# Weights fetched apart from rows, plans ahead of scatters, and places converted when due, in an FFT-then-mixture-of-experts kernel

## The chip, the cores and the metric

The kernel runs on one core of one Trainium2 chip. The metric is the device time of one execution in microseconds (us); less is better. A core has five engines with in-order queues of their own, and they synchronise through semaphores: PE multiplies matrices (PEld is its weight load), DVE and ACT do elementwise work, POOL issues the indirect DMAs here, and SP issues the plain DMAs. All DMAs share 16 DMA engines.

## What is computed

A 2-D Fourier transform of 8 batches of 2496 x 256 numbers, of which the real part is kept, and behind it a top-1 mixture of experts: each of the 19,968 rows goes to the one of 8 experts with the largest gate logit, through two matrix products with a ReLU between, and is scaled by its gate weight.

```
batch, seq, dim = (8, 2496, 256);  N, D, E, F = (19968, 256, 8, 1024)
x = real(fft(fft(x, axis=1), axis=2)).reshape(N, D)
logits = x @ w_gate
e = argmax(logits, axis=1)
gate_w = softmax(logits)[e]
for each expert e, its rows:  y = relu(x @ w1[e]) @ w2[e]
out = gate_w[:, None] * y
```

## The kernel before

Work goes batch by batch through three stages, and the stages of different batches are woven into each other.

*First stage* (`first(b)`): x comes in three pieces per batch (`load`, SP), is folded on DVE (L290 to L301), multiplied by tables on PE (tile s), copied by ACT, and written to a DRAM tensor Td. `regroup` reads it back as tile t4.

*Second stage* (`second(b)`): further products (tiles p, zz) give the transformed rows and their gate logits. After each half batch `route` picks the expert and counts, so that each row gets a place in a DRAM tensor Xs in which every expert has a region: `pf` is the place as a float, `pi` as an integer (L447, L448). For each of the 10 slices of 128 rows it appends an entry to the list `waiting`. `send()` takes one entry from it and issues one indirect DMA on POOL (L230), which writes 128 rows to their places. A batch has 20 such scatters.

*Plan*: once a batch is routed, `close(b)` runs `plan` (L469): some 25 small DVE instructions on one partition, which turn the counts per expert into a table `tab` of blocks: from which row each block starts, and which expert it belongs to. Batch b's blocks are "round" b: two of 256 rows and four of 128 in the first round, four of 256, then three of 512, then five of 512 in each, and in the last round five of 512, seven of 256 and up to 21 of 128 rows.

*Expert blocks* (`experts`, L623): for each block, `fetch` (L517) reads the block's start row and its expert from `tab` into registers of SP and issues three DMAs on SP: the rows (tile xb, from Xs) and the two weights of its expert (w1_sb and w2_sb, both shown as w_sb, 1 MB each). Each has three buffers. `turn` transposes the rows on PE (tile pt) and DVE copies them to xT. The first product (ph, into hT through ReLU on ACT and DVE in turn) and the second (py, scaled by ACT into y, scattered to the output by POOL) follow. The transposes of the next block stand in PE's order between the output products of the current one. Blocks of 512 rows from round 3 on (`halved`) do their first product by seven smaller ones (`seven`, L577, tiles a to e), with extra DVE sums; `Left` makes the sums of weights for it, four DVE instructions (L546).

*What sets the order.* The program is written out in the order in which the engines run it (`manual_schedule`). The loop at L804 weaves: for each batch b from 1 on, `work` yields the blocks of round b-1 in steps (a step has a weight w and says whether PE has its fill), and `side = mixed(b)` is batch b's second stage with the next batch's first stage. After each step that is not "full", side work becomes due at TICKS * w / (SHARE * open_), with TICKS 32 and SHARE 0.65: about so much that 32 steps are done after 65% of the round. For batches below LATE = 4 each side step is followed by one `send()`. From batch 4 on `send()` comes when an allowance `room`, which grows by w per step, reaches ROOM = 1.2.

In `mixed`, a loop waits until `waiting` is empty, and only then does `close(b)` plan the batch. In `experts`, `fetch_some` fetches up to three blocks ahead at the start of a block, and up to two ahead after its first product; it needs the plan and nothing else, since a planned batch has all its scatters issued. DMAs of SP are issued in order, so a fetch of rows that waits for scatters to land keeps the fetches behind it waiting.

Rows that a block reads are ordered behind the scatters of its round's batches by dependency groups (`sent`, `taken`, L235 to L243).

Of the kernel before, what the change touches and what calls it, by code (L numbers as in the profile page):

```python
# [15 lines left out]
ALU = mybir.AluOpType  # L16
# [19 lines left out]
E, F = 8, 1024  # L36
# [145 lines left out]

TICKS = 32
LATE = 4
SHARE, ROOM = 0.65, 1.2
WARM = 16
MOST = max(k for now in rounds() for _, k, _ in now)

# [21 lines left out]
def kernel(ctx: ExitStack, tc, x, w_gate, w1, w2, out):  # L210
    nc = tc.nc
# [51 lines left out]
    con, k = {}, 0  # L263
# [147 lines left out]
    def route(b, h, rows, lg):  # L411

        nonlocal base

        def small(name, *dims, dt=F32):
            return sp.tile([128, *dims], dt, tag=name, name=name)

        mx, eq, v = small("mx", NSL), small("eq", NSL, E), small("v", NSL)
        vec.reduce_max(mx[:], lg[:], axis=AX_X)
        vec.tensor_tensor(eq[:], lg[:], bc(mx[:], 2, E), op=ALU.is_equal)  # L420
        vec.tensor_tensor(eq[:], eq[:], bc(con["rev"][:], 1, NSL), op=ALU.mult)
        vec.reduce_max(v[:], eq[:], axis=AX_X)
# [24 lines left out]
        vec.reduce_sum(pf[:], pos[:], axis=AX_X)  # L447
        vec.tensor_tensor(pi[:], pf[:], con["far"][:, h], op=ALU.add)  # L448
        nxt = cp.tile([128, E], F32, tag="base", name="base", bufs=2)
        vec.tensor_tensor(nxt[:], rk[:, NSL], base[:], op=ALU.add)  # L450
        base = nxt
        for s in range(NSL):
            waiting.append((b, pi[:, s:s + 1], rows[:, s]))

    waiting = deque()

    def send():

        if waiting:
            b, idx, rows = waiting.popleft()  # L460
            sent(put_row(Xs, idx, rows, E * CAP - 1, "xs"), b)


# [50 lines left out]
        yield  # L514
        tabs[b, size, last] = tab

    def fetch(b, size, tab, i):  # L517
        n = size // 128
        row = nc.sync.value_load(tab[:, 0, i:i + 1], min_val=0, max_val=ROWS - size)
        ev = nc.sync.value_load(tab[:, 1, i:i + 1], min_val=0, max_val=E - 1)  # L520
        xb = bp.tile([128, BIG // 128, W], F32, tag="xb", name="xb", bufs=3)
        taken(nc.sync.dma_start(out=xb[:, 0:n].rearrange("p t c -> p (t c)"),
                                in_=Xs[ds(row, size)].rearrange("(p t) c -> p (t c)", t=n)), b)
        w1_sb = bp.tile([128, 2, F], F32, tag="w1", name="w1_sb", bufs=3)
        nc.sync.dma_start(out=w1_sb[:], in_=w1[ds(ev, 1)].rearrange("o p c f -> p (o c) f"))
        w2_sb = bp.tile([128, FC, D], F32, tag="w2", name="w2_sb", bufs=3)
        nc.sync.dma_start(out=w2_sb[:], in_=w2[ds(ev, 1)].rearrange("o p c d -> p (o c) d"))
        return xb, w1_sb, w2_sb

    add, sub = ALU.add, ALU.subtract  # L530

# [22 lines left out]
        vec.tensor_tensor(o[2], b21, o[1], op=sub)  # L554
        return b11, b21, b22, o[2], o[0], o[1], b12

    def turn(b, size, got):


        xb = got[0]  # L560
        xT = bp.tile([128, 2, BIG], F32, tag="xT", name="xT", bufs=1)
        n = min(size // 128, 2)
        for h in range(-(-size // 256)):
            pt = pse.tile([128, 2, n, 128], F32, tag="e", name="pt")
            for c in range(2):
                for t in range(n):
                    nc.tensor.transpose(pt[:, c, t], xb[:, 2 * h + t, c * 128:(c + 1) * 128], ident[:])  # L567
            vec.tensor_scalar(xT[:, :, 256 * h:256 * h + 128 * n], pt[:].rearrange("p c t k -> p c (t k)"),  # L568
                              con["alt"][:], None, op0=ALU.mult)
            yield xT  # L570
        if halved(b, size):
            th = size // 2
            xs = bp.tile([128, 3, th], F32, tag="xs", name="xs", bufs=1)
            r = right(xs, *(xT[:, c, k * th:(k + 1) * th] for c in range(2) for k in range(2)))
            yield r
# [47 lines left out]
    def experts(todo):  # L623
# [1 line left out]

        got, xT, used, left = [], None, None, None

        @contextmanager  # L630
        def needed(last, at, o):
# [11 lines left out]

        def fetch_some(k, most=3):

            while k + len(got) < len(todo) and len(got) < most and todo[k + len(got)][:3] in tabs:
                b, size, last, at = todo[k + len(got)]
                got.append(fetch(b, size, tabs[b, size, last], at))

        for k, (b, size, last, at) in enumerate(todo):  # L650
            n, m = size // 128, BIG // size
            if not k:
                while todo[0][:3] not in tabs:
                    yield 0, False
                fetch_some(0)
                for _ in range(9):
                    yield 0, False
                for xT in turn(b, size, got[0]):
                    pass
            fetch_some(k)  # L660
            xb, w1_sb, w2_sb = got.pop(0)
# [4 lines left out]
            hT = bp.tile([128, FC, BIG], F32, tag="hT", name="hT", bufs=1)  # L666
            more = None
            if follow and got and halved(follow[0], follow[1]):
                more = Left(got[0][1])
# [16 lines left out]
            if follow:  # L686
                while follow[:3] not in tabs:
                    yield 0, False
                fetch_some(k + 1, 2)
                turned = turn(*follow[:2], got[0])  # L690
                if halved(*follow[:2]):
                    left = more or Left(got[0][1])
# [26 lines left out]
    def woven(*parts):  # L719
        parts = list(parts)  # L720
        while parts:
            for p in list(parts):
                if next(p, p) is p:
                    parts.remove(p)
                else:
                    yield

    def close(b):

        for size, k, last in rounds()[b]:  # L730
            yield from plan(b, size, k, last)

    def ahead_of(b):

        yield from first(b)
        regroup(b, 0)
        regroup(b, 1)

    def mixed(b):

        one, two = (ahead_of(b + 1) if b + 1 < B else iter(())), second(b)
        for _ in range(3):
            next(one, None)
            yield
        for k, _ in enumerate(two):
            if k % 2:
                next(one, None)
            yield
        while waiting:
            next(one, None)  # L750
            yield
        yield from woven(close(b), one)

    vec.memset(ones[:], 1.0)
    act.dma_start(out=con["w1"][:, 0:4], in_=waves[:, 0:4])
# [11 lines left out]
    vec.memset(warm[:], 0.0)  # L767
    act.activation(warm[:], warm[:], ACTF.Exp)

    tabs = {}  # L770
    todo = in_order()
    for _ in first(0):
        pass
# [22 lines left out]
    for k, _ in enumerate(second(0)):  # L796
        if k % 2 == 0:
            next(early, None)
        send()
    while waiting:  # L800
        next(early, None)
        send()
    work = experts(todo)
    for b in range(1, B):  # L804

        side, done, due, room = mixed(b), 0, 0.0, 0.0
        if b == 1:
            side = woven(close(0), chain(early, side))
        blocks = [(size, k * size / BIG, halved(b - 1, size)) for size, k, _ in rounds()[b - 1]]
        total = sum(k * (15 if seven_ else 16) for _, k, seven_ in blocks)  # L810
        open_ = sum(k * (8 if seven_ else 16) for _, k, seven_ in blocks)
        while done < total:
            w, full = next(work)
            done += w
            if not full:
                due += TICKS * w / (SHARE * open_) if w else 1
            while due >= 1:
                next(side, None)
                due -= 1
                if b < LATE or not w:  # L820
                    send()
            room = min(room + w, 2)
            if b >= LATE and room >= ROOM:
                send()
                room -= ROOM
        for _ in side:
            send()
# [52 lines left out]
```

## Time and profile before

| what | us |
|---|---|
| median of the runs (lowest) | 1332.57 (1330.49) |
| the profiled execution | 1364.11 |
| its span, first to last instruction | 1362.3 |
| TensorE (PE) busy | 1284.0 |
| first expert product (ph) starts | 92.1 |
| POOL busy with 160 scatters of rows to Xs | 158.7 |
| POOL busy with 163 scatters of output rows | 159.4 |

The profiled execution is 31.5 us longer than the median of the runs, so sums made in the profile are in its own us. The span in 40 slices of 34 us, in tenths of busy time, with the clock that the throttle granted to TensorE and the DMA engines' share:

```profile
PE   6668899899899999999999999999999999999998
POOL 0235215134113411044112521144131111111111
PEclk9869999899999999999999999999999999999999
DMA  8759866644535542454423542232442227777784
```

TensorE is below 90% in the first five slices, where the first batch passes through the first two stages before any block can start, and in a few slices later. The groups of instructions that the change concerns, with count, total busy us, mean ns, and idle time of the engine before them and what ended it:

```profile
L230 POOL DMA_INDIRECT out_dram<-y,ro x163 | 159.4, 978 | 890.6 <-ACT y L702 823.9
L230 POOL DMA_INDIRECT Xs<-rows,pi x160 | 158.7, 992 | 140.1 <-issue 64.3
L567 PE MATMUL pt<-table,xb 128*128 128x128 f32 x326 | 53.3, 279 | 10.8 <-DMA xb<-Xs 9.9
w_sb<-in_moe_w_dram SPq DMA_DIRECT2D x132, 1024.0 KB
xb<-Xs SPq DMA_DIRECT2D x28, 516.0 KB
```

### The profile page before, as it was taken

The numbers are of one execution on the slowest core, as the hardware profiler recorded it, in microseconds if no ns is written. First come the engines' busy times: TensorE is split into PE (matmuls) and PEld (weight loads), VectorE is DVE, ScalarE is ACT, GpSimd is POOL, SyncE is SP. The second block draws the span as 40 slices with busy tenths as digits, with TensorE's granted clock in tenths as the row PEclk, the third lists the DMA queues.
The fourth block names the chain that finished last, engine by engine and source line by source line (L and its number), as shares of the span: only waits on it lengthen the run. The fifth ranks groups of instructions, "written<-read, shape, count | busy, mean of one in ns | idle before, by whom it ended". The sixth has DMA issues, their size and how long they took to land.

```text
span 1362.3 us, 18852 instructions
## 1 busy us (share of the span) xinstructions
PE 1284.0 (94%) x6655; PEld 1103.7 (81%) x6655; DVE 581.0 (43%) x1533; ACT 368.9 (27%) x806; POOL 326.1 (24%) x335
## 2 busy tenths in 40 slices
PE   6668899899899999999999999999999999999998
PEld 4557888576688888887888878888888889999887
DVE  4553244332456465655366554555545421111211
ACT  1322132132134332432234223332223221111111
POOL 0235215134113411044112521144131111111111
PEclk9869999899999999999999999999999999999999
DMA  8759866644535542454423542232442227777784
GB/s 239 250 214 315 294 239 191 250 127 145 226 93 177 195 170 97 134 177 137 174 109 117 201 184 93 94 131 68 177 182 107 89 96 275 260 259 272 267 318 187
DMA packets 63099, 249.62 MB, mean 183 GB/s; under 512 B 10057, under 2 KB 24883, under 8 KB 43420
## 3 DMA queue, kind: packets, MB, share of 16 engines
q1 hardware_dynamic: 46231, 203.33, 42.6%
q0 software_dynamic: 15888, 42.14, 8.5%
q10 hardware_dynamic: 885, 2.94, 0.7%
q8 instruction: 54, 0.88, 0.3%
q14 instruction: 41, 0.34, 0.1%
HBM read 194.97 MB, written 54.83 MB: 183 GB/s over the span
## 4 chain that ended last, share of the span: by engine, by line
PE 87%; DVE 4%; DMA 3%; issue 3%; another core or an unknown queue 1%; ACT 1%; POOL 0%; SPq 0%; POOLq 0%; DVEq 0%; ACTq 0%
PE py L215 40%; PE ph L215 14%; PE a L215 6%; PE c L215 6%; PE p L215 6%; PE b L215 3%; PE d L215 3%; PE pt L567 3%; PE s L215 3%; PE e L215 3%; DMA xq<-in_x_dram 1%; DMA Td<-t 1%; DMA xb<-Xs 1%; DVE hT L606 0%
## 5 line engine op out<-in xcount | busy, mean ns | idle before, releaser
L215 PE MATMUL py<-w_sb,hT 128*128 128x256 f32 x2560 | 580.2, 381 | 6.3 <-DVE hT L682 4.0
L215 PEld LDWEIGHTS py<-w_sb,hT 128*128 128x128 f32 x2560 | 479.2, 191 | 68.0 <-DVE hT L682 4.6
L230 POOL DMA_INDIRECT out_dram<-y,ro x163 | 159.4, 978 | 890.6 <-ACT y L702 823.9
L215 PE MATMUL ph<-xT,w_sb 128*128 128x128 f32 (+2 forms) x1216 | 221.2, 337 | 8.7 <-issue 4.1
L702 ACT ACTIVATE y<-py,xb 128x256 f32<-128x256 f32 x163 | 77.1, 473 | 521.6 <-PE py L215 505.2
L215 PEld LDWEIGHTS ph<-xT,w_sb 128*128 128x128 f32 x1216 | 178.0, 192 | 40.4 <-issue 19.7
L230 POOL DMA_INDIRECT Xs<-rows,pi x160 | 158.7, 992 | 140.1 <-issue 64.3
L682 DVE TENSOR_SCALAR hT<-ph 128x512 f32<-128x512 f32 x63 | 43.5, 691 | 298.5 <-issue 204.1
L600 DVE TENSOR_TENSOR u<-p,b 128x512 f32<-128x512 f32 x50 | 34.4, 688 | 182.3 <-PE b L215 141.1
L215 PE MATMUL a<-xT,w_sb 128*128 128x256 f32 x400 | 103.3, 381 | 5.0 <-ACT p L597 4.3
L215 PEld LDWEIGHTS a<-xT,w_sb 128*128 128x128 f32 x400 | 75.4, 190 | 17.3 <-ACT p L597 5.5
L568 DVE TENSOR_SCALAR xT<-pt,table 128x512 f32<-128x512 f32 (+1 forms) x94 | 63.2, 673 | 46.1 <-PE pt L567 46.1
L403 DVE COPY lg<-p 128x16 f32<-128x16 f32 x80 | 13.9, 173 | 141.9 <-ACT zs L400 129.9
L215 PE MATMUL s<-xq,w 104*112 104x256 f32 (+2 forms) x208 | 61.7, 421 | 12.0 <-DVE xq L292 11.9
L684 ACT ACTIVATE hT<-ph 128x512 f32<-128x512 f32 x63 | 37.6, 597 | 114.2 <-PE ph L215 78.8
L215 PE MATMUL p<-table,zz 128*128 128x145 f32 (+1 forms) x320 | 58.5, 308 | 10.1 <-issue 5.1
L610 ACT ACTIVATE hT<-a 128x512 f32<-128x512 f32 x50 | 29.9, 597 | 137.2 <-PE a L215 117.0
L215 PEld LDWEIGHTS p<-table,t 120*128 120x128 f32 x352 | 53.7, 203 | 12.6 <-issue 9.2
L567 PE MATMUL pt<-table,xb 128*128 128x128 f32 x326 | 53.3, 279 | 10.8 <-DMA xb<-Xs 9.9
L215 PE MATMUL p<-table,t 120*128 120x120 f32 (+1 forms) x352 | 56.1, 287 | 4.4 <-issue 4.4
L567 PEld LDWEIGHTS pt<-table,xb 128*128 128x128 f32 x326 | 38.6, 142 | 25.8 <-DMA xb<-Xs 11.1
L215 PE MATMUL c<-xT,ws 128*128 128x256 f32 x200 | 52.3, 384 | 7.2 <-DVE hT L606 7.2
(113 smaller groups left out, 1266.3 us busy)
## 6 DMA issues: line engine op xcount, KB each, us to landing
w_sb<-in_moe_w_dram SPq DMA_DIRECT2D x132, 1024.0 KB
xq<-in_x_dram SPq DMA_DIRECT2D x24, 896.0 KB
xb<-Xs SPq DMA_DIRECT2D x28, 516.0 KB
Td<-t SPq DMA_DIRECT2D x18, 448.0 KB
t<-Td SPq DMA_DIRECT2D x8, 768.0 KB
t<-Td SPq DMA_DIRECT2D x8, 640.0 KB
xb<-Xs SPq DMA_DIRECT2D x13, 258.0 KB
xb<-Xs SPq DMA_DIRECT2D x25, 129.0 KB
```

The lines of the kernel that those rows point to most:

```text
L215: nc.tensor.matmul(o, lhsT=lhsT, rhs=rhs, start=start, stop=stop, **kw)
L230: return unordered(pool.indirect_dma_start(out=dst, out_offset=bass.IndirectOffsetOnAxis(ap=idx, axis=0), in_=rows, in_offset=None, bounds ...
L403: vec.tensor_copy(lg[:, k:k + 2], p3[:, NY:NY + 2 * E].rearrange("p (m e) -> p m e", m=2))
L567: nc.tensor.transpose(pt[:, c, t], xb[:, 2 * h + t, c * 128:(c + 1) * 128], ident[:])
L568: vec.tensor_scalar(xT[:, :, 256 * h:256 * h + 128 * n], pt[:].rearrange("p c t k -> p c (t k)"), con["alt"][:], None, op0=ALU.mult)
L600: vec.tensor_tensor(u2[:], p1[:], b[:], op=add)
L610: act.activation(h11, a[:], ACTF.Relu)
L682: vec.tensor_scalar(o, ph[:], 0.0, None, op0=ALU.max)
L684: act.activation(o, ph[:], ACTF.Relu)
L702: act.activation(y[:], py[:], ACTF.Copy, scale=xb[:, i, D + 1:D + 2])
```

## The change

1. *Rows and weights are fetched by two functions.* `fetch_weights` needs only the plan. `fetch_rows` needs also that all scatters of the batch are issued, which a new set `whole` tells. `fetch_some` fetches both in turn, and weights may be at most one block ahead of rows.
2. *Plans come ahead of scatters.* `mixed` no longer waits for `waiting` to be empty before `close(b)`; a new step `through(b)` behind it waits and adds b to `whole`. A block whose batch is not whole makes `experts` yield until it is; for batches below 4 such a yield issues all scatters that wait.
3. *Places when due.* From batch 4 on, `route` leaves the place as a float (pf), and `send()` lets ACT convert one column of it to pi just before it issues the scatter.
4. *Two constants.* SHARE goes from 0.65 to 0.6, and from batch 4 on the allowance for scatters grows by 0.75 w instead of w in steps that are not full.

```diff
-SHARE, ROOM = 0.65, 1.2
+SHARE, ROOM = 0.6, 1.2
...
-        vec.tensor_tensor(pi[:], pf[:], con["far"][:, h], op=ALU.add)
+        vec.tensor_tensor(pf[:] if b >= LATE else pi[:], pf[:], con["far"][:, h], op=ALU.add)
...
-            waiting.append((b, pi[:, s:s + 1], rows[:, s]))
+            waiting.append((b, pf[:, s:s + 1], pi[:, s:s + 1], rows[:, s]))
...
-            b, idx, rows = waiting.popleft()
+            b, place, idx, rows = waiting.popleft()
+            if b >= LATE:
+                act.copy(idx, place)
             sent(put_row(Xs, idx, rows, E * CAP - 1, "xs"), b)
...
-    def fetch(b, size, tab, i):
+    def fetch_rows(b, size, tab, i):
         n = size // 128
         row = nc.sync.value_load(tab[:, 0, i:i + 1], min_val=0, max_val=ROWS - size)
-        ev = nc.sync.value_load(tab[:, 1, i:i + 1], min_val=0, max_val=E - 1)
         xb = bp.tile([128, BIG // 128, W], F32, tag="xb", name="xb", bufs=3)
         taken(nc.sync.dma_start(out=xb[:, 0:n].rearrange("p t c -> p (t c)"),
                                 in_=Xs[ds(row, size)].rearrange("(p t) c -> p (t c)", t=n)), b)
+        return xb
+
+    def fetch_weights(tab, i):
+        ev = nc.sync.value_load(tab[:, 1, i:i + 1], min_val=0, max_val=E - 1)
         w1_sb = bp.tile([128, 2, F], F32, tag="w1", name="w1_sb", bufs=3)
...
-        return xb, w1_sb, w2_sb
+        return w1_sb, w2_sb
...
-            while k + len(got) < len(todo) and len(got) < most and todo[k + len(got)][:3] in tabs:
+            while max(len(got), len(xbs)) < min(most, len(todo) - k) or len(xbs) < len(got):
+                n = len(xbs)
+                b, size, last, at = todo[k + n]
+                if (b, size, last) in tabs and b in whole:
+                    xbs.append(fetch_rows(b, size, tabs[b, size, last], at))
+                elif n < len(got):
+                    break
                 b, size, last, at = todo[k + len(got)]
-                got.append(fetch(b, size, tabs[b, size, last], at))
+                if (b, size, last) not in tabs:
+                    break
+                if len(got) <= n:
+                    got.append(fetch_weights(tabs[b, size, last], at))
...
                 while todo[0][:3] not in tabs:
                     yield 0, False
+                fetch_some(0, 1)
+                while b not in whole:
+                    yield 0, True
                 fetch_some(0)
...
                 fetch_some(k + 1, 2)
-                turned = turn(*follow[:2], got[0])
+                while follow[0] not in whole:
+                    yield 0, follow[0] < LATE
+                fetch_some(k + 1, 2)
+                turned = turn(*follow[:2], xbs[0])
...
+    def through(b):
+
+        while waiting and waiting[0][0] == b:
+            yield
+        whole.add(b)
...
-        while waiting:
-            next(one, None)
-            yield
         yield from woven(close(b), one)
+        yield from through(b)
...
-    while waiting:
-        next(early, None)
-        send()
     work = experts(todo)
...
-            side = woven(close(0), chain(early, side))
+            side = woven(chain(close(0), through(0)), chain(early, side))
...
             done += w
+            if full and not w:
+
+                while waiting:
+                    send()
+                whole.add(b - 1)
...
-            room = min(room + w, 2)
+            room = min(room + (w if full else 0.75 * w), 2)
```

More of the change, by code (lines that the diff above doesn't have):

```diff
@@ L555, in right, with turn @@
         return b11, b21, b22, o[2], o[0], o[1], b12
-    def turn(b, size, got):
-        xb = got[0]
+    def turn(b, size, xb):
         xT = bp.tile([128, 2, BIG], F32, tag="xT", name="xT", bufs=1)
@@ L623, in experts @@
     def experts(todo):
-        got, xT, used, left = [], None, None, None
+        xbs, got, xT, used, left = [], [], None, None, None
         @contextmanager
@@ L657, in experts @@
                     yield 0, False
-                for xT in turn(b, size, got[0]):
+                for xT in turn(b, size, xbs[0]):
                     pass
             fetch_some(k)
-            xb, w1_sb, w2_sb = got.pop(0)
+            xb, (w1_sb, w2_sb) = xbs.pop(0), got.pop(0)
             turned = iter(())
@@ L668, in experts @@
             if follow and got and halved(follow[0], follow[1]):
-                more = Left(got[0][1])
+                more = Left(got[0][0])
             if halved(b, size):
@@ L689, in experts @@
                 fetch_some(k + 1, 2)
-                turned = turn(*follow[:2], got[0])
+                while follow[0] not in whole:
+                    yield 0, follow[0] < LATE
+                fetch_some(k + 1, 2)
+                turned = turn(*follow[:2], xbs[0])
                 if halved(*follow[:2]):
-                    left = more or Left(got[0][1])
+                    left = more or Left(got[0][0])
             for i in range(n):
@@ L768 @@
     act.activation(warm[:], warm[:], ACTF.Exp)
-    tabs = {}
+    tabs, whole = {}, set()
     todo = in_order()
```

## The prediction

> **What bounds the kernel now.** I read the page's engine shares first, then TensorE's waits, then busy time by stretch, then the timeline of the stretches in which TensorE stands still.
>
> ```profile
> span 1362.3 us, 18852 instructions
> PE 1284.0 (94%) x6655; PEld 1103.7 (81%) x6655; DVE 581.0 (43%) x1533; ACT 368.9 (27%) x806; POOL 326.1 (24%) x335
> PE pt L567 <- DMA xb<-Xs: 9.9, 2, 6.6
> PE c L215 <- DVE hT L606: 7.2, 9, 1.7
> PE a L215 <- ACT p L597: 4.3, 3, 1.7
> ```
>
> TensorE (PE) is busy 94% of the span and no matmul is removed or added, so the change can only win back idle time and time at a lowered clock: at most the other 6%, 78 us. Most of that is out of reach. The first expert matmul (ph) starts at 92.1 us, after the first transform, a hand-over through DRAM, and 20 scatters of 1.28 us each on POOL. The second to fourth lines (engine, what waits, who releases it: total us, times, longest) show two waits that the diff names: transposes (pt) that wait for rows, and products that wait for ACT or DVE.
>
> The rows first. This is the end of the blocks that run while batch 2 is scattered:
>
> ```profile
> 239.56 0.97 POOL L230 DMA_INDIRECT Xs<-rows,pi  x1 [0.30 <-issue]
> 242.07 0.37 SPq L522 DMA_DIRECT2D xb<-Xs  x1
> 242.64 0.37 SPq L525 DMA_DIRECT2D w_sb<-in_moe_w_dram  x1
> 245.50 1.11 PE L567 MATMUL pt<-table,xb 128*128 128x128 f32 x4 [6.60 <-DMA xb<-Xs]
> ...
> 240.00:245.00 5.00, 0.00 (x0) 0.00 (x0) 0.00 (x0) 0.00 (x0) 0.54 (x1) 0.73 0.49 157
> 245.00:250.00 5.00, 4.50 (x15) 3.83 (x16) 0.75 (x1) 0.00 (x0) 0.00 (x0) 0.59 1.00 420
> 350.00:355.00 5.00, 4.07 (x13) 3.37 (x14) 0.75 (x1) 0.00 (x0) 0.00 (x0) 0.66 1.01 410
> ```
>
> Timeline lines give start, duration, engine and, in brackets, the idle time before; stretch lines give length, busy time of PE, PEld, DVE, ACT, POOL, granted clock, DMA share, GB/s. The last scatter ends at 240.5, the rows are asked for at 242.1 and the weights behind them, the transposes start at 245.5, and PE, which had no other work, lost 6.6 us and then ran at a granted clock of 0.59. The same happens a round later, at 347.6 (3.3 us, clock 0.66).
>
> Now the small waits later on:
>
> ```profile
> 628.08 0.97 POOL L230 DMA_INDIRECT Xs<-rows,pi  x1 [0.30 <-issue]
> 629.36 0.97 POOL L230 DMA_INDIRECT Xs<-rows,pi  x1 [0.30 <-issue]
> 630.63 0.97 POOL L230 DMA_INDIRECT Xs<-rows,pi  x1 [0.30 <-issue]
> 633.16 0.58 ACT L597 COPY p<-a 128x512 f32<-128x512 f32 x1 [1.54 <-PE c L215]
> 633.80 1.13 PE L215 MATMUL a<-xT,w_sb 128*128 128x256 f32 x4 [1.66 <-ACT p L597]
> ...
> 427.00:1000.00 573.00, 558.97 (x2833) 485.58 (x2832) 310.85 (x765) 187.72 (x396) 158.53 (x162) 1.00 0.42 147
> ```
>
> From 427 to 1000 us PE idles 573.0 - 559.0 = 14.0 us. Every idle spot over 0.2 us (near 448, 477, 604, 633, 760, 790, 912, 940, 997) stands within or at most 5 us behind a run of four or more scatters back to back on POOL, during which ACT and DVE start 1 to 2 us after the matmul they are put down to has ended. That is a correlation; why a run of scatters holds ACT and DVE up the trace does not say.
>
> **The change part by part.** Reference: the profiled execution, 1364.1 us (span 1362.3), which is 2.4% above the median of the runs, 1332.57. I sum in the profile's us and scale.
>
> 1. *Plan ahead of the scatters, rows and weights apart, side work earlier (0.65 to 0.60).* No instruction of weight is added: the same plans, the same 132 weight and 66 row transfers. What moves is order. In the emitted order the second half of batch 2 is routed 3.4 us of PE work sooner (151.2 to 147.8 on a count of matmul columns at 216 ns per 256 columns and two passes, the pace of py in the chain: 3.46 us for 16), its plan 11 us sooner, and only one scatter is left after the next-to-last output row instead of three plus one. Three scatters less there are 3 x 1.28 = 3.8 us (1.28 from start to start, as 628.08 to 629.36 above); I take the last scatter to end 3.5 to 5 us sooner, near 236. The rows need 3.4 us from issue (242.07 to 245.50) and 1.6 from scatter end to issue: 236 + 5 = 241 against 238.9, when PE arrives. The wait falls from 6.6 to about 2.1, **4.5 us**. The restart ran 16 py in 4.75 us instead of 3.46 and pt in 0.9 instead of 0.44: another **1.8**. Who is late next: nobody behind PE, since the first weights now go before the rows.
> A rule of the Trainium skill speaks against this one: DMA: Bandwidth & Descriptors, "Anatomy of one DMA", says each DMA engine shares itself in turn between the queues that have work. The early weights (2 x 1024 KB) then share with the last scatters. The row beside it: 220 to 230 us already shows a DMA share of 0.95 to 0.97, but 230 to 240 only 0.21 to 0.26, and 420 GB/s was reached at 245. Two MB at that pace are 5 us; asked for near 224, they are through before the last scatters of 233 to 236. With the row I charge nothing; by the rule in its worst form the scatters end 2 us later and this part gives 4.3 instead of 6.3. I keep 6.3 and put 2 us in the range.
>
> 2. *Next round boundary (347.6).* The plan ran at 337.9 to 346, after the scatters, on DVE between hT copies; rows were asked for at 347.3. Now they are asked for at the start of the last block, as soon as the scatters land (about 341). PE arrives at 347.6: the 3.3 us wait goes, and 0.95 + 0.52 us of waits for hT at 337 and 341.7, which stood in the plan's neighbourhood, by half. Clock: 1.7 us (half speed for 3.4 us). Sum **5.7**. Here TensorE: Matmul & The Clock Gate, "Part 1: The HAM clock gate", gives about 3.4 us of idleness as what halves the clock: by it alone a 3.3 us wait might cost no clock, and this part would be 4.0. The measured 0.66 after just this wait decides. The 2.1 us left at the first boundary should cost none: waits of 1.7 and 2.3 us near 125 and 131 left the granted clock at 1.00.
>
> 3. *Places when due, and the slower allowance (0.75 per step outside the seven products).* From batch 4 on a scatter cannot start before ACT has converted its place, and ACT reaches that conversion in step with its own work. Runs of six (emitted together after an output row in before) become groups of three, one, two, one with 2 to 3 us of matmuls between. Of the 14.0 us idle in 427 to 1000, 2.1 us (at 996 to 999) belong to the pad scatters, which are not touched. Of 11.9 I take two thirds: **8.0**. Bounds: 0 if the runs are not the cause, 11.9 if all.
> Cost: 80 copies of one column on ACT. Nearest row: the copies of 5 or 6 columns at L367, 170 ns: 80 x 0.17 = 13.6 us of ACT, which is 67% idle in this stretch (187.7 of 573). Behind each copy in ACT's order stand the copy of a and the Relus that PE needs; bounds 0 and 13.6, I take **-1.0**. POOL now waits for ACT where it waited for DVE; the outputs queued behind it have six y buffers. DVE is unchanged (pf instead of pi, 170 ns).
>
> 4. *The first block.* Its weights are asked for when its plan is ready (about 72 us, DMA share 0.2 to 0.3 then) instead of at 86.7. Rows still wait for the last scatter (85.9). They landed 3.9 us after issue beside 2 MB of weights; alone I take 2.4: **1.5**. Bounds 0 and 2.
>
> Sum: 6.3 + 5.7 + 8.0 - 1.0 + 1.5 = 20.5 us; 1364.1 - 20.5 = 1343.6, times 1332.57/1364.1 = **1312 us**.
>
> **The rivals.**
> *More than that (chance 0.27).* From 120 to 150 us PE is busy 21.95 of 30 us, 8.05 lost, at a DMA share of 0.89, with ACT and DVE idle up to 10.9 us for a reason that the trace puts to "remote". Two MB of weights moved from 87 to 72 thin out the queue of transfers that leads up to it. If that was the cause, 20.5 + 8.05 = 28.5 us: 1335.6, scaled 1305. Against: the transfers of this stretch itself are issued at 121 to 139 and are the same.
> *Only the boundaries (0.17).* POOL's runs only coincide with the waits, or the grouped copies let the runs happen again: part 3 gives 0 to -1. 12.5 us are left: 1351.6, scaled 1320. This is also the case in which the change does not spread what it means to spread.
> *ACT turns into the bound (0.06), slower.* Place: the seven products of batches 4 to 7, where product a waits for ACT's copy of a (already 4.3 us in three waits). Price: 80 copies, each in front of such a copy or of a Relu. Before its own cost the sum is 21.5: from 0.27 us per copy (21.5/80) all of it is gone, which is over its own 170 ns and so needs queueing as well; or, with part 3 void, from 0.17 (13.5/80). At 0.35 us each and part 3 void, 28 - 13.5 = 14.5 us more: about 1379, scaled 1347. For it: ACT is in order, and its chain is what PE waits for. Against: 67% idle.
>
> **How the numbers follow.** The forecast itself has 0.50. Faster by over 2% (below 1305.9; 2% is about what a measurement of this kernel can tell from no change) holds most of the first rival and the upper end of the forecast, where bursts give all 11.9 and the restart costs nothing: 0.25 + 0.10 = 0.35. Slower by over 2% (above 1359): only the end of the last rival, 0.03. Within: 0.62. Range: the first rival with some more of the waits before 92 us, 1297, to a little beyond "only the boundaries", 1327.
>
> **What would show it.** The wait of pt for xb near 239 should be under 3 us and the one near 348 gone, both with granted clock near 1.0. The sum of PE idle in the five later rounds should fall from 14.0 to about 6, with no more than three scatters back to back there. ACT busy should rise by about 14 us with its waits by PE unchanged. If the stretch 120 to 150 is also full, the first rival is right. I am wrong if PE's idle spots remain though the scatters are spread, or if a new wait of PE for ACT p appears.

## The result, and the profile after

Kernel before and changed kernel ran in turn on one chip, six executions each. The changed kernel's median is 1321.03 us (1318.04 to 1322.44), that of before there 1331.38 us (five of the six from 1329.07 to 1332.57; one took 1944.71 us, and the record does not say why). The ratio is 0.9925, with a 95% interval of 0.9908 to 0.9941: 10.4 us less, a gain that the interval separates from zero. The forecast was 1312 us; the measured time lies inside its range, 9 us from its middle, and the gain is about half of the 20 us that were forecast.

The profiles tell of a larger step than the runs do. The changed kernel's profiled execution, 1322.44 us, is one of its six. The profiled execution of before, 1364.11 us, is none of the six beside it; it took 32.7 us more than their median, and on which chip it ran is not on record. So the spans differ by 41.6 us and the medians by 10.4. Three quarters of what the two traces show as won is no gain of this comparison, and the section on the experiments is mostly about finding out what it is.

The page of the changed kernel: span, busy time of each engine, and TensorE and its granted clock in 40 slices.

```profile
span 1320.7 us, 19014 instructions
PE 1277.2 (97%) x6655; PEld 1106.3 (84%) x6655; DVE 582.3 (44%) x1533; ACT 374.4 (28%) x886; POOL 329.5 (25%) x335
PE   5769999999999999999999999999999999999998
PEclk9869999999999999999999999999999999999999
```

From the fourth slice on TensorE is busy for 90% or more of each slice but the last. Its idle time fell from 78.3 us (1362.3 - 1284.0) to 43.5 us (1320.7 - 1277.2), and it needed 6.8 us less for the same 6655 matmuls, which is put down here to less time at a lowered clock. ACT has the 80 copies that the change adds, and is busy 5.5 us longer.

The boundary between the first and the second round of blocks (near 239 us in before), in the timeline:

```profile
210.60 0.97 POOL L230 DMA_INDIRECT Xs<-rows,pi  x1 [0.30 <-issue]
212.47 0.60 ACT L700 ACTIVATE hT<-ph 128x512 f32<-128x512 f32 x1 [2.86 <-PE ph L215]
...
228.04 1.52 SPq L523 DMA_DIRECT2D xb<-Xs  x2
231.29 0.66 PE L571 MATMUL pt<-table,xb 128*128 128x128 f32 x4 [2.88 <-DMA xb<-Xs]
```

The rows are asked for at 228.0 and the transposes start at 231.3, after 2.88 us of idleness in place of 6.60. The last scatter to Xs starts at 223.38 and ends at 224.35: from its end to the request for rows 3.7 us go by, where the forecast took 1.6 from before. A second thing is to be seen in the first two lines: ten scatters to Xs run back to back from 209 to 222 us (one of the ten lines is shown), and ACT takes its product as soon as TensorE has it (the wait before it ends with ph). Nothing is held up behind this run of scatters.

The same kernel in stretches. Columns: stretch and length, busy time of PE, PEld, DVE, ACT and POOL with instructions, granted clock, DMA share, GB/s.

```profile
120.00:150.00 30.00, 30.00 (x191) 27.75 (x190) 5.80 (x19) 4.28 (x8) 14.25 (x15) 1.00 1.02 394
230.00:235.00 5.00, 3.71 (x14) 3.11 (x15) 0.75 (x1) 0.00 (x0) 0.00 (x0) 0.76 0.89 290
330.00:360.00 30.00, 30.00 (x146) 26.24 (x145) 17.60 (x30) 8.03 (x15) 3.89 (x4) 1.00 0.50 199
427.00:1000.00 573.00, 572.43 (x2904) 502.85 (x2904) 314.58 (x757) 190.90 (x461) 159.11 (x159) 1.00 0.41 143
```

Second line: the wait of 2.88 us is followed by a clock of 0.76 in the mean of this stretch; cut into half microseconds, the trace shows 0.50 from 232.5 to 236 us. Third line: at the next boundary, where before waited 3.30 us near 348, nothing is lost. Fourth line: of 14.0 us of idle time in the later rounds 0.57 us are left. First line: from 120 to 150, where before lost 8.05 us, TensorE is full.

The scatters of the later rounds, in the timeline:

```profile
573.45 1.29 POOL L230 DMA_INDIRECT Xs<-rows,pi  x1 [2.83 <-ACT pi L462]
575.05 0.97 POOL L230 DMA_INDIRECT Xs<-rows,pi  x1 [0.30 <-issue]
576.33 0.97 POOL L230 DMA_INDIRECT Xs<-rows,pi  x1 [0.30 <-issue]
579.49 1.30 POOL L230 DMA_INDIRECT Xs<-rows,pi  x1 [2.19 <-ACT pi L462]
```

POOL waits for the place that ACT converts (L462), and so runs of scatters end after three. Between 427 and 1000 us before has eight runs of six or seven; the changed kernel has none longer than three.

One difference is not in the kernel. In before's trace DVE and ACT have waits that are put to "remote", 45.0 us over the whole execution (what stands behind "remote" the trace does not say). The two largest in the waits view of before (total us, times, longest):

```profile
DVE hT L682 <- remote: 17.3, 2, 10.9
ACT hT L684 <- remote: 13.0, 2, 9.4
```

The changed kernel's trace has not a microsecond of such waits.

### The profile page after: what moved, and what is told of

The parts are those of the page before. It is cut to its first block, busy times and chain, and to the rows that moved or that the text cites. A ratio compares the mean times of both kernels' runs of the same rounds, so it can differ in the third digit from the quotient of the medians.

```text
span 1320.7 us, 19014 instructions
## 1 busy us (share of the span) xinstructions
PE 1277.2 (97%) x6655; PEld 1106.3 (84%) x6655; DVE 582.3 (44%) x1533; ACT 374.4 (28%) x886; POOL 329.5 (25%) x335
## 5 line engine op out<-in xcount | busy, mean ns | idle before, releaser
L230 POOL DMA_INDIRECT Xs<-rows,pi x160 | 162.1, 1013 | 173.6 <-DVE rows L405 53.0
L698 DVE TENSOR_SCALAR hT<-ph 128x512 f32<-128x512 f32 x63 | 43.5, 691 | 297.2 <-issue 204.9
L215 PE MATMUL p<-table,t 120*128 120x120 f32 (+1 forms) x352 | 58.8, 292 | 1.3 <-ACT t L367 1.1
L215 PEld LDWEIGHTS s<-xq,w 104*112 104x112 f32 x208 | 39.5, 207 | 22.7 <-DVE xq L292 10.8
```

The lines of the kernel that those rows point to most:

```text
L215: nc.tensor.matmul(o, lhsT=lhsT, rhs=rhs, start=start, stop=stop, **kw)
L230: return unordered(pool.indirect_dma_start(out=dst, out_offset=bass.IndirectOffsetOnAxis(ap=idx, axis=0), in_=rows, in_offset=None, bounds ...
L698: vec.tensor_scalar(o, ph[:], 0.0, None, op0=ALU.max)
```

## The experiments

Two theories stood at the start. The profiled execution of before is typical of it, and the change removes its stalls (P in the expectations). Or the profiled execution was an odd one, and before without its stalls takes 1330 us (Q). Besides, it was open which part of the change gains: order of plans and fetches, the places, or SHARE. Each set of kernels ran on one chip, together with before on the same chip; there were three sets on three chips, and not every kernel ran in each. Ratios are against that before, with 95% intervals.

**First set: before again, and the parts.** Before, unchanged.

> The kernel before, unchanged, profiled once more. Theory P (the first profile of before shows what every execution of it does): a span near 1362 us again, with about 14 us of PE idle in the five later rounds. Theory Q (that one execution was disturbed; its stalls from 117 to 150 us and behind the scatter runs are mostly its own): a span near 1330 us, with less than half of those stalls, and only the waits of pt for xb left as in the first profile.

Measured: 1374.06 us, ratio 1.0009 (0.9987 to 1.0031), span 1372.7. On this chip before takes 3% more than in the first comparison (1373.3 against 1331.4), in all its runs, and its trace shows the stalls again: 57.8 us of "remote" waits on ACT and DVE, and pt waiting for rows 7.17 and 3.24 us. So the stalls are no accident of one execution, and a before that takes 1330 us was not met here.

The changed kernel without the places, on the chips of the first and of the second set:

```diff
-        vec.tensor_tensor(pf[:] if b >= LATE else pi[:], pf[:], con["far"][:, h], op=ALU.add)
+        vec.tensor_tensor(pi[:], pf[:], con["far"][:, h], op=ALU.add)
...
-            if b >= LATE:
-                act.copy(idx, place)
...
-            room = min(room + (w if full else 0.75 * w), 2)
+            room = min(room + w, 2)
```

> The changed kernel without its part 3: places are converted by DVE for all batches, no copies on ACT, and the allowance grows by w. Theory P: the runs of scatters come back and PE idles 8 to 12 us more in the later rounds, about 1331. Theory Q: the runs cost little in ordinary executions, about 1321 to 1324, as the changed kernel (1321.0).

Measured: 1359.05 us, 0.9902 (0.9873 to 0.9931).

The places alone, put into before:

```diff
-        vec.tensor_tensor(pi[:], pf[:], con["far"][:, h], op=ALU.add)
+        vec.tensor_tensor(pf[:] if b >= LATE else pi[:], pf[:], con["far"][:, h], op=ALU.add)
...
+            if b >= LATE:
+                act.copy(idx, place)
...
-            room = min(room + w, 2)
+            room = min(room + (w if full else 0.75 * w), 2)
```

> The kernel before with part 3 alone (places converted on ACT from batch 4 on, allowance 0.75 w). Theory P: 8 to 12 us faster than before, about 1321. Theory Q: within 3 us of before, 1328 to 1332; the 80 copies on ACT may take back what is gained.

Measured: 1353.97 us, 0.9867 (0.9836 to 0.9899). The later rounds, first in before on this chip and then with the places alone:

```profile
427.00:1000.00 573.00, 556.40 (x2809) 482.34 (x2809) 306.31 (x758) 185.89 (x393) 155.06 (x159) 1.00 0.41 143
427.00:1000.00 573.00, 570.12 (x2903) 500.60 (x2902) 317.38 (x771) 195.21 (x479) 166.79 (x166) 1.00 0.42 149
```

TensorE's idle time there falls from 16.6 to 2.9 us. (The traced execution with the places, 1344.89 us, is the fastest of its six; that of before, 1374.44 us, is near its median.) The part has two changes in it, the copies on ACT and the slower allowance; no run separates them.

The changed kernel with the old SHARE (`SHARE, ROOM = 0.65, 1.2`):

> The changed kernel with SHARE 0.65 as before. If the 3.4 us by which a batch is routed sooner carry the first boundary, the wait of pt for xb near 228 us grows from 2.9 to about 6 us and the time by 3 to 5 us, to 1325. If plan and fetch order carry it, it stays within 1.5 us of 1321.

Measured: 1349.19 us, 0.9826 (0.9795 to 0.9858). The changed kernel itself came to 0.9815 on the chip of the third set, whose before is as slow (1373.5): SHARE is worth nothing that these intervals show. The trace tells more of it than the time. With the old SHARE three scatters and one again stand behind the last output rows, as in before, the last of them at 244.4 us, and the wait for rows is back:

```profile
246.87 1.52 SPq L523 DMA_DIRECT2D xb<-Xs  x2
250.16 1.12 PE L571 MATMUL pt<-table,xb 128*128 128x128 f32 x4 [5.29 <-DMA xb<-Xs]
```

With the new SHARE and without the places, on the same chip, one scatter stands there, the rows are asked for at 238.3 and pt does not wait. So the earlier end of the scatters at the first boundary comes from SHARE, and not from the order of plans and fetches alone.

Each part gains by itself on this chip: 14.3 us the order of plans and fetches (with the new SHARE), 19.3 us the places. Together they would be 33.6; the whole change gains 24.1 with the old SHARE here. Both parts in part remove the same stalls: without the places, idle time from 427 to 1000 us already falls from 16.6 to 9.4 us.

**Second set: does the gain hang on the chip?** The rivals now were that the change gains the same everywhere (S), and that it gains more where scatters hold up ACT and DVE (R). The changed kernel, unchanged:

> The changed kernel once more, beside a before of the same chip. Chips differ: before took 1331 on the chip of the first comparison and 1373 on the second. Theory R (scatter runs hold up ACT and DVE on one kind of chip and not on the other): where before takes about 1373 this takes about 1347 (ratio 0.98, since plan and fetch order alone gave 0.990 and places alone 0.987 there); where it takes about 1331, 1321 (0.9925). Theory S (the gain is the same everywhere): 0.9925 on any chip.

Measured: 1346.69 us against 1364.27, ratio 0.9884 (0.9865 to 0.9902), 17.6 us less. The interval does not touch that of the first comparison (0.9908 to 0.9941); S falls. This chip's before is the nearest to the profile from which the forecast was made:

> One look at the kernel before on the same chip, for its profile. Theory R: if the runs are near 1331, PE idles under 3 us from 427 to 1000 us and hardly from 117 to 150; if near 1373, about 14 us and 8 us as in the two profiles so far. The waits of pt for xb near 239 and 348 stand in both.

Its time was 1366.71 us, its span 1364.9, with 45.0 us of "remote" waits, as many as in the first profile. It shows what before does where the changed kernel also was traced. Before on this chip, stretches:

```profile
120.00:150.00 30.00, 22.52 (x111) 18.93 (x110) 6.55 (x27) 2.61 (x5) 15.06 (x16) 0.90 0.87 300
200.00:260.00 60.00, 53.37 (x261) 44.98 (x261) 20.82 (x76) 11.97 (x29) 25.29 (x26) 0.94 0.69 241
330.00:360.00 30.00, 25.69 (x75) 15.04 (x75) 9.53 (x31) 3.33 (x6) 7.98 (x9) 0.89 0.51 200
427.00:1000.00 573.00, 558.58 (x2830) 485.33 (x2828) 310.13 (x764) 186.59 (x394) 158.75 (x162) 1.00 0.42 147
```

The changed kernel on the same chip:

```profile
120.00:150.00 30.00, 26.01 (x143) 22.37 (x142) 6.52 (x22) 3.21 (x6) 14.80 (x16) 0.94 0.94 336
200.00:260.00 60.00, 49.70 (x239) 41.72 (x238) 16.73 (x60) 9.72 (x23) 22.89 (x24) 0.89 0.58 203
330.00:360.00 30.00, 27.57 (x100) 17.62 (x99) 8.13 (x14) 4.29 (x8) 8.66 (x10) 1.00 0.56 214
427.00:1000.00 573.00, 570.35 (x2903) 500.49 (x2902) 315.73 (x772) 194.89 (x479) 165.64 (x165) 1.00 0.43 148
```

In the later rounds (fourth line) TensorE's idle time falls from 14.4 to 2.65 us, much as in the first comparison. But from 200 to 260 (second line) it loses 10.3 us, more than the 6.6 of before, and from 120 to 150 it loses 4.0 although in the first comparison the same kernel lost nothing. The timeline shows what stands there:

```profile
222.28 0.98 POOL L230 DMA_INDIRECT Xs<-rows,pi  x1 [0.30 <-issue]
223.49 0.60 ACT L700 ACTIVATE hT<-ph 128x512 f32<-128x512 f32 x1 [7.88 <-remote]
224.14 3.78 PE L215 MATMUL ph<-xT,w_sb 128*128 128x256 f32 x8 [5.59 <-issue]
...
231.89 0.69 DVE L698 TENSOR_SCALAR hT<-ph 128x512 f32<-128x512 f32 x1 [14.26 <-remote]
232.64 3.54 PE L215 MATMUL ph<-xT,w_sb 128*128 128x256 f32 x8 [4.72 <-DVE hT L698]
```

POOL issues scatters back to back from 212 to 229.7 us. TensorE's ph of 214.9 to 218.6 (before the lines shown) is done, yet ACT takes it at 223.5 and DVE at 231.9, and the next ph waits twice, 5.59 and 4.72 us. In the first comparison a like run of scatters (209 to 222) held nobody. The load of the DMA engines does not tell the two apart: their busy share is 1.07 and 1.03 from 220 to 230 us here, and 1.05 from 210 to 220 there.

There is no wait of pt for rows left in this trace, but not for the reason that was forecast:

```profile
244.64 1.52 SPq L523 DMA_DIRECT2D xb<-Xs  x2
250.26 0.60 PE L571 MATMUL pt<-table,xb 128*128 128x128 f32 x4
```

The last scatter (at 242.1) stands behind an output row that was itself late, and the rows are asked for at 244.6, where before on this chip asks at 242.2. TensorE does not wait for them because the held engines have made it later still: it comes to pt at 250.3, and in before at 239.0.

Without the places on this chip:

> The changed kernel without part 3, again. On a chip where before takes 1373: ratio 0.990, part 3 being worth about 12 us there. Where before takes 1331, theory R expects 1321 to 1323, as the changed kernel, since there are no stalls behind scatter runs to be won back; theory S expects 1331 or more.

Measured: 1355.39 us, 0.9942 (0.9924 to 0.9961): 8.9 us. From 427 to 1000 its busy time is

```profile
427.00:1000.00 573.00, 566.62 (x2868) 493.56 (x2867) 315.18 (x771) 187.02 (x397) 163.25 (x163) 1.00 0.42 147
```

so 6.4 us are idle, with four runs of six scatters and four of five in this stretch. Of the 11.8 us by which the whole change shortens this idle time, 8.0 come without the places.

If runs of scatters are what holds ACT and DVE, then places when due should be worth it from the first batch on:

```diff
-        vec.tensor_tensor(pf[:] if b >= LATE else pi[:], pf[:], con["far"][:, h], op=ALU.add)
+        vec.tensor_tensor(pf[:] if b else pi[:], pf[:], con["far"][:, h], op=ALU.add)
...
-            if b >= LATE:
+            if b:
                 act.copy(idx, place)
...
-    for _ in work:
-        next(rest, None)
+    for k, _ in enumerate(work):
+        if k % 4 == 0:
+            next(rest, None)
```

(The last lines spread the pad scatters of the last round, the 2.1 us near 997.)

> The changed kernel with places converted on ACT from batch 1 on instead of 4, and the pad scatters at every fourth step. Theory R: on a chip where before takes 1373, the stalls of 1 to 5 us behind scatter runs in rounds 0 to 2 and the 2 us at the pads go as well, 6 to 10 us faster than after_again; where before takes 1331 no gain, or 1 to 3 us slower, for scatters that start later let the rows of rounds 1 to 3 come later. Theory S: the same small change on any chip.

Measured: 1337.78 us, 0.9816 (0.9799 to 0.9834), 8.9 us below the changed kernel on the same chip, intervals apart. Its stretches:

```profile
120.00:150.00 30.00, 22.47 (x110) 19.02 (x109) 6.22 (x24) 3.29 (x15) 14.76 (x15) 0.89 0.83 304
200.00:260.00 60.00, 56.57 (x280) 46.39 (x281) 22.55 (x82) 14.88 (x52) 25.56 (x26) 1.00 0.75 262
427.00:1000.00 573.00, 572.43 (x2907) 502.36 (x2906) 320.10 (x766) 196.29 (x474) 162.46 (x163) 1.00 0.43 149
```

From 200 to 260, where the scatters of batch 2 are now paced, TensorE's loss is 3.4 us in place of 10.3. From 120 to 150 nothing is won: the loss is 7.5 us, with scatters in runs of six and four from 119 us on. The later rounds give 0.57 us of idle time in place of 2.65. The third set shows how far the first of these readings carries.

**Third set: are the early weights what holds the engines?** The first blocks' weights, 2 MB, now move while scatters run. In this kernel they wait for the scatters as the rows do:

```diff
-                if (b, size, last) not in tabs:
+                if (b, size, last) not in tabs or b not in whole:
                     break
```

> The changed kernel with weights asked for only when the batch is whole, behind the rows; plans stay ahead, places as changed. Theory T (on a chip where before takes 1360 or more, weights that are loaded while a run of scatters goes out are what holds ACT and DVE, 5.6 + 4.7 us near 218 to 232 in the changed kernel): these two stalls vanish, the wait of pt for xb comes back at 3 to 6 us near 230, and the time is 3 to 6 us below after_third. Theory U (the early weights are worth what the forecast said, 1.5 us at the first block and some of the boundary): 2 to 4 us above after_third. Where before takes 1331 there are no such stalls, and this is 1 to 4 us above after_third on either.

Measured: 1345.15 us, 0.98 (0.9758 to 0.9842). The changed kernel beside it:

> The changed kernel on this chip, to set the others against. Theory R: ratio 0.988 where before takes about 1364, 0.98 where about 1373, 0.9925 where about 1331.

Measured: 1347.93 us, 0.9815 (0.9774 to 0.9857). The two cannot be told apart. In the kernel with late weights the stalls behind scatters remain (4.12 us near 236, 3.74 near 333, 6.06 near 125), as they do in before, whose weights are late too; so the early weights are not their cause. The wait of pt for rows that theory T expected does not come back. And ph at the first block has a wait that the changed kernel has not:

```profile
86.26 0.60 PE L571 MATMUL pt<-table,xb 128*128 128x128 f32 x4
89.45 1.97 PE L215 MATMUL ph<-xT,w_sb 128*128 128x256 f32 x8 [2.58 <-DMA w_sb<-in_moe_w_dram]
```

It costs 2.58 us at this spot and nothing that the times show.

Places from the first batch on, once more, and the same with late weights:

> places_all again, beside after_third. Where before takes 1360 or more: 7 to 10 us below after_third, as on the third chip. Where before takes 1331: within 3 us of after_third, since there the scatter runs stall nobody.

Measured: 1344.29 us, 0.9769 (0.9725 to 0.9812). That is 3.6 us below the changed kernel, with intervals that overlap; on the second chip it was 8.9, clear of them. The traces of this set turn the reading of 200 to 260 round. Places from batch 1:

```profile
200.00:260.00 60.00, 51.70 (x260) 44.41 (x259) 19.68 (x72) 13.03 (x48) 24.93 (x26) 0.94 0.65 226
```

and the changed kernel:

```profile
200.00:260.00 60.00, 55.82 (x268) 45.44 (x267) 20.49 (x69) 11.88 (x29) 24.52 (x26) 0.97 0.72 244
```

Here the paced kernel loses 8.3 us and the changed one 4.2. What a run of scatters costs at this boundary differs from one execution or chip to the next by more than the two kernels differ. The 3.4 against 10.3 above is therefore no proof that pacing helps there. Steady is only the gain of some 2.5 us in the later rounds (table below), where the changed kernel still waits for 2 us at the pad scatters near 981 and this one does not; where the rest of the 8.9 us came from is open.

> weights_wait with places on ACT from batch 1 on and spread pad scatters. If the two act on different stalls, the gains add: places_all was 9 us below after_again, so by theory T some 12 to 15 us below after_third. If both act on the same stall near 220, no better than places_all_2.

Measured: 1341.46 us, 0.9768 (0.9728 to 0.9808): late weights again make no difference.

**Where each kernel spends its time.** ACT scales 163 tiles of output rows (y). Cutting each trace at the 25th and at the 109th of them gives three stages with the same output work in each (us):

| kernel (set) | up to the 25th | 25th to 109th | rest | ratio |
|---|---|---|---|---|
| before, first profile | 356.8 | 646.7 | 358.8 | 1 |
| before (second set) | 357.2 | 647.3 | 360.4 | 1 |
| without places (second set) | 356.0 | 640.2 | 358.5 | 0.9942 |
| changed (second set) | 354.8 | 631.8 | 358.5 | 0.9884 |
| places from batch 1 (second set) | 346.6 | 629.3 | 358.5 | 0.9816 |
| before (first set) | 357.9 | 654.3 | 360.5 | 1 |
| without places (first set) | 349.4 | 644.6 | 358.6 | 0.9902 |
| places alone (first set) | 353.1 | 631.1 | 358.8 | 0.9867 |
| changed (third set) | 350.3 | 631.9 | 358.5 | 0.9815 |
| places from batch 1 (third set) | 354.7 | 629.3 | 359.1 | 0.9769 |
| changed, first comparison | 332.8 | 629.3 | 358.6 | 0.9925 |

The kernel with the old SHARE and the two with late weights, which the table leaves out, stand in the same columns: 348 to 357 and 629 to 632 us. The cuts are read from lines like these, before on the chip of the second set:

```profile
357.21 0.47 ACT L702 ACTIVATE y<-py,xb 128x256 f32<-128x256 f32 x1 [11.40 <-PE py L215]
1004.48 0.47 ACT L702 ACTIVATE y<-py,xb 128x256 f32<-128x256 f32 x1 [2.81 <-PE py L215]
```

and the changed kernel on the same chip:

```profile
354.75 0.47 ACT L721 ACTIVATE y<-py,xb 128x256 f32<-128x256 f32 x1 [5.01 <-PE py L215]
986.51 0.47 ACT L721 ACTIVATE y<-py,xb 128x256 f32<-128x256 f32 x1 [2.80 <-PE py L215]
```

Read down the middle column: with the places it is 629 to 632 us in every kernel on every chip, without them 640 to 654. Read down the first: 346 to 358 wherever scatters hold up ACT and DVE, whatever the kernel, and 332.8 where they do not. Each row is one execution, and two traces of one kernel differ by up to 8 us (346.6 and 354.7 in the first column, 647.3 and 654.3 in the second), so only large steps are to be read; the 332.8 us are those of a single trace.

## Why the prediction was right, and where it was not

**The total.** The time fell into the range, and the gain was half of the forecast's. The sum in the profile's own microseconds was 20.5. On the chip whose before agrees with that profile (1364.27 us to 1364.11) the change saved 17.6, and on the chip of 1373.5 it saved 25.6. In the comparison it saved 10.4. The step that most likely failed is the last one, "times 1332.57/1364.1": it takes the 31.5 us between profile and runs for a factor on everything. In the first comparison the changed kernel shows no wait behind scatters at all, and the sum contains a large term, part 3, that is made of such waits alone. Leaving part 3 out leaves 12.5 us, the rival "only the boundaries", and 1320; the measured 1321.03 us lies there. For this rival's reading speaks that the changed kernel's trace there has no held engines. But there is no trace of a before that took 1331 us, so how the 10.4 us divide there is argued and not shown.

**Part 1, first boundary (6.3 us).** The forecast took the wait of pt from 6.6 to about 2.1; it became 2.88 in the first comparison. There the scatters ended as early as was hoped, but the rows were asked for 3.7 us behind the last of them instead of 1.6; with 1.6 the wait would have been under 1 us (estimate from the lines above). On the other chips it vanished, on the second by luck: TensorE came later than the rows. The run with the old SHARE shows which part of the change did it here, the 0.60. "The 2.1 us left at the first boundary should cost none" of the clock was wrong at the value that came: after 2.88 us the granted clock was 0.76 from 230 to 235. So this wait, too, lowered the clock from below the 3.4 us of the rule weighed at part 2, and the row was the better guide again. "Who is late next: nobody behind PE" was wrong on the chips with held engines. ACT and DVE were late next, behind the same scatters: from 200 to 260 us TensorE lost 10.3 us on the second chip, in place of 6.6, and 4.2 on the third, so that the gain of the vanished wait was given back wholly there and in part here.

**Part 2, second boundary (5.7 us).** Here the mechanism is the one that was forecast: on the second chip the rows are asked for at 340.7 us in place of 346.6. The wait near 348 is gone in each trace of the changed kernel, the clock from 330 to 360 is 1.00 in all three, and in the first comparison the stretch of 330 to 360 is full. On the second chip 2.4 us are still lost there, against 4.3 in before.

**Part 3, places when due (8.0 less 1.0).** The correlation that it rested on held when it was acted on: before with nothing but this part takes 23.2 us less between the 25th and the 109th tile (654.3 to 631.1), and no run of scatters is longer than three from 427 to 1000. The size was too small for the chips with held engines: idle time from 427 to 1000 fell by 11.8 us (14.4 to 2.65), the upper bound that was named, not two thirds of it, and the whole stage by 15.5 (647.3 to 631.8). But not all of it is part 3's, as the forecast had it: without the places the idle time there falls by 8.0 us already, and the runs of seven scatters are gone; the sum had put nothing into these rounds for parts 1 and 2. On the second chip the later rounds nearly make up for the boundaries: the stage up to the 25th tile brought 2.5 us where parts 1, 2 and 4 had 13.5. The total there was near, with its terms wrong in opposite directions.

**The copies on ACT.** 80 copies at 170 ns were put at up to 13.6 us of ACT. A copy takes 192 ns in the median, yet ACT's busy time rises by 5.5 us (by 5.1 on the second chip), not by the 14 that were named as a sign, and the waits of TensorE for p are gone: this rival had no hold. Why the rise is smaller than 80 copies is not shown.

**Part 4, the first block (1.5 us).** In the first comparison the rows of the first block land 2.7 us after their issue, where before took 3.9. But on the second chip ph starts at 89.57 us in before and at 89.58 in the changed kernel: nothing was won there. With late weights a wait of 2.58 us appears at the first block, and the time does not change. The term was within its bounds, and no time shows it.

**The rule on shared DMA engines.** In the Trainium skill it stands in DMA: Bandwidth & Descriptors under "Queues, rings and completion order", not under the section that the forecast names. It was charged nothing, against up to 2 us for the scatters next to early weights. The two kernels with late weights are level with those with early ones, within intervals of about 0.4% (some 6 us) to each side; a difference of 2 us is below that. One trace speaks for it: in the first comparison the early weights, asked for at 209.8 and 212.7, move while the scatters do (DMA share 1.05 from 210 to 220, 0.90 from 220 to 225), and the rows are asked for 2.1 us later behind the last scatter than was taken. If the weights are the cause, charging nothing was too little there; that it is the weights and not other transfers no run shows.

**"More than that."** The stretch 120 to 150 is indeed full in the first comparison. But it is 26.0 of 30 us in the same kernel on the second chip, beside 22.5 in before, and 24.5 on the third. So of the 8.05 us about 3.5 go to the change where engines are held, and a full stretch was no sign that this rival is right.

**What stays open.** Why one chip holds ACT and DVE behind back-to-back scatters and another does not, whether it is the chip or its neighbours at the time, whether the copies or the slower allowance spread the scatters, and what before spends where on an undisturbed one. The best kernel of the study, places from batch 1, was not run on a chip of the first kind; what it gains there is not known.

## What to carry to other kernels

Compare the profiled execution with the timed runs before adding up stalls from it: if it is longer, ask which stalls could be the difference, and give terms that rest on them a chance of zero instead of scaling every term. Long runs of back-to-back scatters on one queue are worth breaking up by letting each wait for a small step of an engine whose pace one trusts; here it cost 5.5 us of an engine with room, and took 8 us (640.2 to 631.8, beside the other changes) to 23 us (654.3 to 631.1, alone) from a stage in which ACT and DVE were held up behind scatters. Where they were not, its gain is not known. Where a wait for data is gone, check that the data came sooner, and not the engine later, and look at which other engine works past the same point and could be late next.

## What the runs showed of the hardware

- On three chips (before at 1364 to 1374 us) ACT and DVE stood idle behind runs of scatters, spaced 1.28 us, in waits put to "remote": 38 to 71 us an execution, in every kernel traced there. At the boundary shown above they had been idle for 7.88 and 14.26 us when they took products that TensorE had ended at 218.6 us. In the first comparison the changed kernel had 0.0 us of such waits, with runs of scatters as long.
- The same program thus differed by 3% between the first comparison and these chips (medians of 6 to 19 executions), and the changed kernel by 2% (1321.03 to 1347.93).
- Idleness of TensorE of 2.88 us was followed by a granted clock of 0.50 for 3.5 us. Shorter waits went both ways: 2.33 us left it at 1.00 (before, 131 us), 2.35 us was followed by 0.51 from 342 to 345 us (without the places, second set).
